# Layer pair 1 in seven products on pairs of token blocks, weight sums kept in DRAM

## The chip, the cores and the metric

One core of a Trainium2 chip runs the whole program. The metric is device time in microseconds (us) of that core; lower is better. The kernel before takes 1819.49 us, the median of three runs (1819.48 to 1819.55).

## The reference

Attention over pooled keys, then two gated layer pairs on its output, all in float32:

```
k_p, v_p = mean over 8 neighbouring positions of k, v   # 576 -> 72 keys
attn = softmax(q @ k_p^T / 8) @ v_p                     # batch 8, heads 8, head size 64
x = attn as 4608 tokens x 512
y = ((x @ w_a) * (x @ w_b)) @ w_out                     # 512 -> 1536 -> 512  (layer pair 1)
h = y @ w_in                                            # 512 -> 2048         (layer pair 2)
out = (h * clip(h + 3, 0, 6) / 6) @ w_out2              # 2048 -> 512
```

q, k and v come as float32, the weights as float64; the kernel decodes each weight from its two 32-bit halves.

## The kernel before

4608 tokens are 9 blocks of 512. Layer pair 1 is one loop over blocks j and over f, the 12 tiles of 128 columns of `w_a` and `w_b` (`step`, L670). x lies transposed: 4 chunks of 128 features on the partitions, 512 tokens in the free dimension, as a high part `xh` (float32r) and a low part `xl`; every weight tile is split in the same way. A product of two split numbers is three matmuls (`mm3`, L510): high x high, low x high, high x low. So a step is 4 chunks x 3 matmuls for `pa`, the same for `pb`, and 4 x 3 for y of the step before (`y_part`): 36 matmuls of 128x128 on 512 columns. y stays in four PSUM banks over the 12 f of a block and leaves them once (`y_store`). ScalarE copies `pa` and `pb` to SBUF (L695, L708), GpSimd multiplies them (L713), ScalarE rounds the product to its high part and GpSimd subtracts (L73, L74). Block 0 works in plain float32, four-pass matmuls; in it the weights are decoded. In block 1 they are split and stored to DRAM (`w1dram`), and from block 2 on loaded again at every step, `AHEAD = 3` steps ahead (L507).

Attention runs between the steps. A block has 4 or 5 chunks of up to 128 query rows; each has its transposes, scores, softmax, a second transpose and, for a piece of one or two chunks, the product with v (`pv`, L345), which writes `xh` and `xl`. Every one of these calls stands in a slot; there are 3 slots a step, 36 a block (`plan`, `at`, `place`), and `base` gives the slot at which a chunk begins: the chunks of block j run during block j - 1. From block 3 on the weights of layer pair 2 are staged too, an item per two steps (`w2_stage`, `w2_decode`, `w2_end`).

The order is the one in which the program is written (`manual_schedule`); every engine works through its own instructions in that order. All DMAs are issued by SP's queue (SyncE), in that order too: one that waits for its data, or for its slot in a pool, holds the ones behind it. A pool tag has a fixed number of slots; `wpool` has 28 of 4 KB per partition and serves weights, raw q and k and, in layer pair 2, nearly everything.

Layer pair 2 already works in seven products on two blocks at once: h and f are split in halves, `in_prod` computes the products 1, 2, 6, 5, 7, 3, 4 in three PSUM banks (Z, W, X), with sums of weights from DRAM (`wsd`) and sums of y made in the last pair of the superblock before (`s_make`), and `out_chunk` adds the output in SBUF (L865) after every pair of f tiles.

Of the kernel before, what the change touches and what calls it, by code (L numbers as in the profile page):

```python
# [25 lines left out]
def pooled_attention_then_two_moe_kernel(  # L26
# [34 lines left out]
    xpool = ctx.enter_context(tc.tile_pool(name="xpool", bufs=2))  # L61
    gpool = ctx.enter_context(tc.tile_pool(name="gpool", bufs=2))
    spool = ctx.enter_context(tc.tile_pool(name="spool", bufs=2))
# [6 lines left out]
    ydram = [dpool.tile([P, NCC, TB], F32, name=f"ydram{j}") for j in range(NB)]  # L70

# [34 lines left out]
    def x_tiles(j):  # L106
        if j not in xh_t:
            xh_t[j] = xpool.tile([P, NCC, TB], F32R if j else F32, tag="xh", name=f"xh{j}")
            xl_t[j] = xpool.tile([P, NCC, TB], F32R, tag="xl", name=f"xl{j}") if j else None
        return xh_t[j], xl_t[j]  # L110

    def load_tile(b, shape, name):


        if b == 0 or b >= 3:
            return wpool.tile(shape, F32, tag="w", name=name)
        return ld.tile(shape, F32, tag="ld", name=name)
# [8 lines left out]
    kpool, vpool = {}, {}  # L126

# [217 lines left out]
    def pv(pi, g):  # L345
# [11 lines left out]
        xh, xl = (x[:, 2 * g : 2 * g + 2, r : r + N] if x is not None else x for x in x_tiles(j))  # L357
# [24 lines left out]
    SLOTS = 3 * NF1  # L382
    plan = {}
# [4 lines left out]
    base = []  # L388
    for j in range(NB):
        n = len(block_chunks[j])  # L390
        for i, c in enumerate(block_chunks[j]):
            if j == 0:
                base.append(None)
            elif j == 1:
                base.append(4 * i + 6)
            else:
                base.append(SLOTS * (j - 1) - 8 + i * SLOTS // n)
    att_used = {}

# [10 lines left out]
    for c, (b, t0, n) in enumerate(chunks):  # L410
        pi, off = chunk_piece[c]
        s0 = base[c]
        near = b < 3
        if c in block_chunks[0]:
            continue
        if t0 == 0:
# [7 lines left out]
            for g in range(2):  # L424
                at(dma_at[1][g], v_dma, b, g)
                at(v_at[g], v_prep, b, g)
                at(v_at[g] + 1, v_write, b, g)
# [7 lines left out]
        if b == 0:  # L435
            place(s0, (q_tr, c))
        else:
            at(s0, q_tr, c)
        x = place(max(s0, done) + 1, (scores, c, 0), (scores, c, 1))
        at(x + 1, expo, c)  # L440
        at(x + 2, sums, c)
        at(x + 3, normal, c)
        x = place(x + 5, (at_main, c), (at_left, c))
        if off + n == pieces[pi][2]:
            for g in range(2):
                x = place(max(x + 1, s0 + 10 + g), (pv, pi, g))

    def run_slot(s):
        for fn, args in plan.pop(s, ()):
# [66 lines left out]
    def layer_in(o, w, xh, xl):  # L516
        for c in range(NCC):
            s = slice(c * P, (c + 1) * P)
            if xl is None:
                nc.tensor.matmul(o, w[:, s], xh[:, c], start=c == 0, stop=c == NCC - 1)  # L520
                continue
            mm3(o, w[:, 0, s], w[:, 1, s], xh[:, c], xl[:, c], c == 0, c == NCC - 1)


    yacc, later = {}, []
# [14 lines left out]
    def y_store(j, half):  # L540


        if j == NB - 1:
            t = wpool.tile([P, 2, TB], F32, tag="w", name="yl")
            nc.scalar.copy(t[:, 0], yacc[j][2 * half])
            nc.vector.tensor_copy(t[:, 1], yacc[j][2 * half + 1])
            nc.sync.dma_start(ydram[j][:, 2 * half : 2 * half + 2], t)
            return
        for c in (2 * half, 2 * half + 1):
            yo = spool.tile([P, TB], F32, tag="io", name="yo", bufs=2)  # L550
# [22 lines left out]
    def w2_decode(i):  # L573
        w2st[i] = w2st[i], spool.tile([P, 512], F32, tag="wst", name="w2f")
        decode_begin(w2st[i][1], w2st[i][0])
        decode(w2st[i][1], w2st[i][0])
# [93 lines left out]
    def step(j, f):  # L670
# [5 lines left out]
        i = NF1 * (j - 3) + f  # L676
        staged = i // 2 - 1 if 2 < i < 4 * NF2 + 2 and i % 2 else None
        stores, later[:] = list(later), []
        if j == 0:
            if f + 3 < NF1:  # L680
                w1_dma(f + 3)
        nj, nf = divmod(NF1 * j + f + 1, NF1)
# [4 lines left out]
        if 2 <= lj < NB:  # L687
            w1_load((lj, lf), lf, 0)
            w1_load((lj, lf), lf, 1)
        if 0 <= i < 4 * NF2 and i % 2 == 0:  # L690
            w2_stage(i // 2)
# [319 lines left out]
```

## Time and profile before

| | |
|---|---|
| median of the runs | 1819.49 us |
| the profiled execution: span | 1818.9 us |
| TensorE / VectorE / ScalarE / GpSimd busy | 1781.3 / 956.1 / 726.9 / 750.9 us |
| DMA | 328.71 MB, 181 GB/s over the span |

Busy times are those of one profiled execution. A matmul's record reaches past the start of the next one, so the time that a matmul costs is read from the distance of starts. "Idle before" is the time that an engine stood still just before an instruction, and the name behind it is what ended that. PEclk is the granted clock of TensorE as a share of 2.4 GHz.

### The profile page before, as it was taken

What the parts mean: (1) busy time and instruction counts of PE and PEld (TensorE: products, weight loads), DVE (VectorE), ACT (ScalarE), POOL (GpSimd) and SP (SyncE); (2) the same over time, 40 slices, a digit from 0 to 9 for tenths busy, and PEclk for the clock granted to TensorE, in tenths of its full rate; (3) what the DMA queues carried; (4) which work ended last, traced back from release to release, by engine and by line L of the source; (5) the groups of instructions that cost most, each with busy time, mean ns of one, the idle gap of its engine ahead of it and who ended that gap; (6) DMA issues with size and microseconds to landing.
All of it is one profiled execution on the core that took longest, in us unless ns stands there. A gap on an engine that the chain in (4) does not pass through costs nothing.

```text
span 1818.9 us, 23423 instructions
## 1 busy us (share of the span) xinstructions
PE 1781.3 (98%) x8148; PEld 1435.3 (79%) x8148; DVE 956.1 (53%) x1617; ACT 726.9 (40%) x1389; POOL 750.9 (41%) x653
## 2 busy tenths in 40 slices
PE   5999999999999999999999999999999999999998
PEld 4444788888888888888888878888888888888897
DVE  6787644323455345454332366685447445644645
ACT  4454443323333334333333355445325433433443
POOL 4545554333444444444343357464225223422322
PEclk8999999999999999999999999999999999999999
DMA  9652356635646548565545467556446543644483
GB/s 248 183 167 53 123 171 212 209 109 157 238 150 201 199 153 262 169 202 188 196 157 203 165 232 268 197 181 219 138 139 205 173 149 124 212 152 153 148 294 127
DMA packets 196260, 328.71 MB, mean 181 GB/s; under 512 B 86320, under 2 KB 107824, under 8 KB 196144
## 3 DMA queue, kind: packets, MB, share of 16 engines
q1 hardware_dynamic: 196144, 327.22, 55.2%
q8 instruction: 65, 1.06, 0.2%
q14 instruction: 51, 0.42, 0.1%
HBM read 264.24 MB, written 62.91 MB: 180 GB/s over the span
## 4 chain that ended last, share of the span: by engine, by line
PE 90%; DVE 5%; ACT 1%; issue 1%; SPq 0%; DMA 0%; POOL 0%; DVEq 0%; ACTq 0%
PE o L512 7%; PE o L513 7%; PE o L514 7%; PE pa L512 5%; PE pb L512 5%; PE pa L514 5%; PE pa L513 5%; PE y L512 5%; PE pb L513 5%; PE pb L514 5%; PE y L514 5%; PE y L513 5%; PE phZ L512 3%; PE phZ L513 3%; PE phZ L514 3%; PE sc L258 2%
## 5 line engine op out<-in xcount | busy, mean ns | idle before, releaser
L74 POOL TENSOR_TENSOR g<-r,g 128x512 fp32r<-128x512 f32 (+1 forms) x160 | 197.8, 1246 | 425.5 <-ACT g L73 255.9
L865 DVE TENSOR_TENSOR oacc<-o,oacc 128x512 f32<-128x512 f32 x252 | 172.3, 688 | 135.2 <-PE o L514 135.0
L713 POOL TENSOR_TENSOR asb<-asb,bsb 128x512 f32<-128x512 f32 x96 | 126.1, 1314 | 250.8 <-ACT bsb L708 217.7
L513 PE MATMUL o<-wo,g 128*128 128x512 f32 x576 | 224.4, 390 | 0.0
L514 PE MATMUL o<-wo,g 128*128 128x512 f32 x576 | 224.2, 389 | 0.0
L512 PE MATMUL o<-wo,g 128*128 128x512 f32 x576 | 211.6, 390 | 1.4 <-ACT g L73 1.2
L695 ACT COPY asb<-pa 128x512 f32<-128x512 f32 x108 | 63.3, 586 | 275.2 <-PE pa L514 231.0
L74 POOL TENSOR_TENSOR gl<-asb,gh 128x512 fp32r<-128x512 f32 x96 | 128.6, 1340 | 107.0 <-ACT gh L73 105.4
L512 PE MATMUL pa<-xh,wa 128*128 128x512 f32 x384 | 152.8, 398 | 0.0
L514 PE MATMUL pa<-xl,wa 128*128 128x512 f32 x384 | 149.8, 390 | 0.0
L513 PE MATMUL pa<-xh,wa 128*128 128x512 f32 x384 | 149.6, 390 | 0.0
L846 ACT ACTIVATE r<-hs 128x512 f32<-128x512 f32 (+1 forms) x120 | 69.0, 590 | 165.3 <-DVE hs L896 163.0
L708 ACT COPY bsb<-pb 128x512 f32<-128x512 f32 x108 | 63.3, 586 | 176.7 <-PE pb L514 149.3
L512 PEld LDWEIGHTS o<-wo,g 128*128 128x128 f32 x576 | 107.5, 188 | 23.9 <-ACT g L73 2.4
L514 PEld LDWEIGHTS o<-wo,g 128*128 128x128 f32 x576 | 108.2, 188 | 22.1
L513 PEld LDWEIGHTS o<-wo,g 128*128 128x128 f32 x576 | 108.2, 188 | 22.1
L512 PE MATMUL phZ<-Sh,wi 128*128 128x512 f32 (+1 forms) x320 | 117.5, 368 | 1.2 <-DVE hs L896 1.2
L513 PE MATMUL phZ<-Sh,wi 128*128 128x512 f32 (+1 forms) x320 | 117.7, 368 | 0.0
L73 ACT CAST g<-r 128x512 fp32r<-128x512 f32 (+1 forms) x160 | 91.9, 579 | 62.7 <-DVE r L847 62.6
L514 PE MATMUL phZ<-Sl,wi 128*128 128x512 f32 (+1 forms) x320 | 114.6, 368 | 0.0
L847 DVE SCALAR_TENSOR_TENSOR r<-r,hs 128x512 f32<-128x512 f32 (+1 forms) x120 | 92.5, 788 | 27.0 <-ACT r L846 26.7
L87 POOL TENSOR_TENSOR w2f<-w2f,w2st 128x512 int32<-128x512 int32 x32 | 42.5, 1328 | 135.7 <-DVE w2f L86 93.9
(1361 smaller groups left out, 4170.7 us busy)
## 6 DMA issues: line engine op xcount, KB each, us to landing
wi<-wsd SPq DMA_DIRECT2D x96, 512.0 KB
wo<-wod SPq DMA_DIRECT2D x64, 512.0 KB
wsd<-wi SPq DMA_DIRECT2D x24, 512.0 KB
kraw<-in_k_dram SPq DMA_DIRECT2D x32, 288.0 KB
out_dram<-oacc SPq DMA_DIRECT2D x36, 256.0 KB
vraw<-in_v_dram SPq DMA_DIRECT2D x32, 256.0 KB
ydram<-yo SPq DMA_DIRECT2D x32, 256.0 KB
w2st<-in_moe_w_in_dram SPq DMA_DIRECT2D x16, 512.0 KB
```

Source lines behind the costliest of these rows:

```text
L73: (hi_eng or nc.scalar.copy)(hi, src)
L74: (lo_eng or nc.gpsimd).tensor_tensor(lo, src, hi.bitcast(F32), ALU.subtract)
L87: nc.gpsimd.tensor_tensor(di, di, lo.bitcast(I32), ALU.add)
L512: nc.tensor.matmul(o, wh, xh, start=first, stop=False, skip_group_check=more)
L513: nc.tensor.matmul(o, wl, xh, start=False, stop=False, skip_group_check=more)
L514: nc.tensor.matmul(o, wh, xl, start=False, stop=last, skip_group_check=more)
L695: nc.scalar.copy(asb, pa)
L708: nc.scalar.copy(bsb, pb)
L713: nc.gpsimd.tensor_tensor(asb, asb, bsb, ALU.mult)
L846: nc.scalar.activation(r[:, :n], src, AF.Relu, bias=3.0)
L847: nc.vector.scalar_tensor_tensor(r[:, :n], r[:, :n], 6.0, src, ALU.min, ALU.mult)
L865: nc.vector.tensor_tensor(acc, o, acc, ALU.add)
```

## The change

Blocks 0, 1 and 2 (`PLAIN = 3`) stay as they are. Blocks 3 to 8 become three superblocks of two blocks (1024 tokens), and their gates are computed as in layer pair 2. The two halves of a superblock are its blocks; the 512 features are split in halves, and the 12 f tiles are taken in six pairs (p, p + 6). For each of the seven products `x_prod` runs twice, for `w_a` and for `w_b`, 6 matmuls each. The Z banks use the PSUM tag that `pa` and `pb` had, W, X and the y chunks share the four banks that y had.

- The sums of weights are made once by `t_make` in slots 48 to 114 (blocks 1 and 2 and the first steps of superblock 0): per pair seven casts on ScalarE, four sums on VectorE and seven subtractions, a third of them on GpSimd; 42 tiles of 0.5 MB go to DRAM (`tdram`). The decoded weights take a turn through DRAM for it (`abdram`).
- A tile of sums is loaded for every product, `LEAD = 3` products ahead (`ab_load`); `w_out` once per pair.
- x of blocks 3 to 8 goes to DRAM as attention makes it (`x_store`), without the subtraction for the low part, and comes back as four half tiles (`x_load`), from which `x_make` makes the seven sums with their low parts: for superblock 0 in slots 99 to 110, for the others during the last pair of the superblock before.
- y is no longer summed over f in PSUM: after each pair, eight chunks of 6 matmuls are evicted and added in SBUF by VectorE (`y_chunk`), spread over the next pair's products by `YWORK`.
- The slots of a pair are 12, one or two behind each half product (`hook`). Attention of blocks 3 and 4 now begins in slots 45 to 79, of 5 and 6 in 97 to 148, of 7 and 8 in 154 to 218, with one slot more between its parts. Staging of an item of layer pair 2 takes 6 slots.
- The first operands of layer pair 2 are made in the last pair of superblock 2 (`y_load` and two sums 16 slots before its end), in place of the last six steps of block 8.
- `xpool`, `gpool` and `spool` have one tag each, with 8, 7 and 4 slots.

The core of the diff:

```diff
+    SPAN2 = (26, 41)
+    SPANS = ((45, 79), (97, 148), (154, 218))
+    T_AT = [*range(48, 57), 72, *range(75, 82), *range(83, 90), *range(91, 98), *range(99, 106), *range(107, 115)]
...
+            for n, i in enumerate((1, 2, 4, 6, 5, 3, 7)):
+                if held:
+                    low()
+                t = wpool.tile([P, 2, 2, 256], F32R, tag="w", name=f"tt{p}_{i}")
+                nc.scalar.copy(t[:, 0], src[i])
+                if i in sums:
+                    nc.vector.tensor_tensor(*sums[i])
+                held = t, src[i], i
...
+    def x_evict(s, p, i):
+        za, zb_ = xb["Za"], xb["Zb"]
+        if i in (1, 6, 5):
+            for m in "ab":
+                xk[i, m] = tmp(F32, f"k{i}{m}")
+                nc.scalar.copy(xk[i, m], xb[("X" if i == 5 else "Z") + m])
+        due = split_due.pop() if split_due else None
+        if i in (2, 7, 3):
+            k, bank, key = {2: (1, "W", (0, 0)), 7: (5, "Z", (1, 1)), 3: (6, "X", (0, 1))}[i]
+            ta, tb = xk.pop((k, "a")), xk.pop((k, "b"))
+            nc.vector.tensor_tensor(ta, xb[bank + "a"], ta, ALU.add)
+            nc.vector.tensor_tensor(tb, xb[bank + "b"], tb, ALU.add)
+            nc.gpsimd.tensor_tensor(ta, ta, tb, ALU.mult)
+            split_due.append(((s, p) + key, ta))
+        elif i == 4:
+            ta = tmp(F32, "k4")
+            nc.scalar.copy(ta, za)
+            nc.vector.tensor_tensor(ta, zb_, ta, ALU.mult)
+            split_due.append(((s, p, 1, 0), ta))
+        if due:
+            key, t = due
+            g = wpool.tile([P, 2, TB], F32R, tag="w", name="g1")
+            split(g[:, 0], g[:, 1], t)
+            g1_t[key] = g
+
+    def y_chunk(s, p, h, c):
+        o = ps_acc.tile([P, TB], F32, tag="acc", name="y1")
+        cs = slice(c * P, (c + 1) * P)
+        for fi in range(2):
+            g, w = g1_t[s, p, fi, h], wo1_t[s, p][fi]
+            mm3(o, w[:, 0, cs], w[:, 1, cs], g[:, 0], g[:, 1], fi == 0, fi == 1)
...
+            (nc.scalar.copy if c % 2 else nc.vector.tensor_copy)(acc, o)
+        else:
+            nc.vector.tensor_tensor(acc, o, acc, ALU.add)
...
+    YWORK = (1, 1, 2, 1, 1, 1, 1)
...
+        for q, i in enumerate(ORDER):
+            n = 7 * (NP1 * s + p) + q
+            ab_load(n + LEAD)
+            if q == 0:
+                wo1_load(s, p)
+            if p == NP1 - 2 and q == 6 and not last:
+                x_load(s + 1)
+            x_prod(s, p, i, 0)
+            hook()
+            x_prod(s, p, i, 1)
+            x_evict(s, p, i)
...
+            for _ in range(YWORK[q] if work else 0):
+                y_chunk(*work.pop(0))
+            hook()
```

## Rows read from the trace of the kernel before

**Rows 1.** The page: span, and busy us (share) x instructions of each engine.
```profile
span 1818.9 us, 23423 instructions
PE 1781.3 (98%) x8148; PEld 1435.3 (79%) x8148; DVE 956.1 (53%) x1617; ACT 726.9 (40%) x1389; POOL 750.9 (41%) x653
```

**Rows 2.** The page: the chain that ended last, shares by engine.
```profile
PE 90%; DVE 5%; ACT 1%; issue 1%; SPq 0%; DMA 0%; POOL 0%; DVEq 0%; ACTq 0%
```

**Rows 3.** Busy us by stretch: PE, PEld, DVE, ACT, POOL; clock, DMA share, GB/s.
```profile
424.00:531.00 107.00, 105.92 (x505) 87.96 (x504) 47.25 (x95) 38.23 (x78) 43.10 (x40) 1.00 0.64 198
534.00:967.00 433.00, 431.78 (x2092) 359.49 (x2092) 193.43 (x390) 156.20 (x316) 187.26 (x167) 1.00 0.59 193
```

**Rows 4.** Timeline of TensorE: start us, us, then the matmul; three gate matmuls.
```profile
753.84 0.47 PE L512 MATMUL pb<-xh,sp(6, 0)_0_6628 128*128 128x512 f32 x1
...
966.96 0.39 PE L512 MATMUL pb<-xh,sp(7, 11)_0_8608 128*128 128x512 f32 x1
...
975.12 0.39 PE L512 MATMUL pb<-xh,sp(8, 0)_0_8674 128*128 128x512 f32 x1
```

**Rows 5.** VectorE by line and form: busy us, mean ns | idle before, its releaser.
```profile
L865 DVE TENSOR_TENSOR oacc<-o,oacc 128x512 f32<-128x512 f32 x252 | 172.3, 688 | 135.2 <-PE o L514 135.0
...
L91 DVE SCALAR_TENSOR_TENSOR w2f<-w2st,w2f 128x512 uint32<-128x512 uint32 x32 | 42.6, 1330 | 13.0 <-POOL w2f L87 12.9
...
L74 DVE TENSOR_TENSOR Sl<-yb,Sh 128x1024 fp32r<-128x1024 f32 x17 | 26.6, 1567 | 4.3 <-ACT Sh L73 4.0
...
L331 DVE TENSOR_TENSOR atl<-atm,ath 128x512 fp32r<-128x512 f32 x32 | 22.1, 692 | 103.5 <-ACT ath L330 103.3
...
L896 DVE TENSOR_TENSOR hs<-phW,kgl 128x512 f32<-128x512 f32 x32 | 22.0, 688 | 27.0 <-ACT kgl L891 13.1 <-ACT r L846 7.2 <-PE phW L514 6.7
...
L86 DVE TENSOR_SCALAR w2f<-w2f 128x512 uint32<-128x512 uint32 x32 | 13.7, 428 | 1.1
...
L85 DVE TENSOR_SCALAR w2f<-w2f 128x512 f32<-128x512 f32 x32 | 13.5, 422 | 106.2 <-ACT w2f L79 106.0
...
L74 DVE TENSOR_TENSOR wi<-sums,wi 128x512 fp32r<-128x512 f32 x9 | 9.2, 1034 | 0.5 <-ACT wi L73 0.5
...
L824 DVE TENSOR_TENSOR yT<-yb,yT 128x1024 f32<-128x1024 f32 x1 | 1.4, 1421 | 0.8 <-DMA yb<-ydram 0.8
...
L74 DVE TENSOR_TENSOR sp(1, 5)_1_2066<-raw,sp(1, 5)_1_2066 128x512 fp32r<-128x512 f32 x1 | 1.4, 1371 | 1.5 <-ACT sp(1, 5)_1_2066 L73 1.5
...
L74 DVE TENSOR_TENSOR sp(1, 6)_1_2142<-raw,sp(1, 6)_1_2142 128x512 fp32r<-128x512 f32 x1 | 0.7, 691 | 0.0
```

**Rows 6.** Busy times by 50 us: block 0, and the start of layer pair 2.
```profile
100.00:150.00 50.00, 47.59 (x159) 24.78 (x158) 40.88 (x82) 23.97 (x48) 26.69 (x25) 1.00 0.54 155
...
1050.00:1100.00 50.00, 48.77 (x216) 40.06 (x215) 32.23 (x37) 28.60 (x52) 31.33 (x27) 1.00 0.72 267
...
1200.00:1250.00 50.00, 49.85 (x220) 40.95 (x219) 36.87 (x43) 26.93 (x41) 26.77 (x15) 1.00 0.62 205
```

**Rows 7.** Busy times by 10 us, for the DMA's share and rate (the last two numbers).
```profile
590.00:600.00 10.00, 10.00 (x51) 8.07 (x50) 7.15 (x17) 5.02 (x12) 2.96 (x3) 1.00 0.48 100
600.00:610.00 10.00, 10.00 (x46) 8.29 (x45) 1.68 (x4) 2.97 (x5) 5.98 (x7) 1.00 0.98 361
```

**Rows 8.** GpSimd and ScalarE by line and form.
```profile
L74 POOL TENSOR_TENSOR gl<-asb,gh 128x512 fp32r<-128x512 f32 x96 | 128.6, 1340 | 107.0 <-ACT gh L73 105.4 <-DVE vraw L132 1.6
L713 POOL TENSOR_TENSOR asb<-asb,bsb 128x512 f32<-128x512 f32 x96 | 126.1, 1314 | 250.8 <-ACT bsb L708 217.7 <-PE y L514 21.0 <-PE sc L258 11.8
...
L891 ACT COPY kgl<-phX 128x512 f32<-128x512 f32 x32 | 18.7, 583 | 14.9 <-PE phX L514 14.7
```

**Rows 9.** Timeline of SP's queue: start us, us that the issues took, xcount.
```profile
539.92 7.73 SPq L223 DMA_DIRECT2D qraw<-in_q_dram  x16
...
689.42 7.39 SPq L182 DMA_DIRECT2D vlraw<-in_v_dram  x6
...
699.07 13.18 SPq L223 DMA_DIRECT2D qraw<-in_q_dram  x16
```

More of the change, by code (lines that the diff above doesn't have):

```diff
@@ L126, in pooled_attention_then_two_moe_kernel, with flush, x_store @@
     kpool, vpool = {}, {}
+    x_done, xo_due, xo_t, later = {}, [], {}, []
+    def flush():
+        for dst, src in later:
+            nc.sync.dma_start(dst, src)
+        later.clear()
+    def x_store():
+        if xo_due:
+            nc.sync.dma_start(*xo_due.pop(0))
     def sum8(dst, t, eng=None):
@@ L386, in at, with spread @@
         plan.setdefault(slot, []).append((fn, args))
[L388 to L397, printed above, removed]
+    def spread(cs, first, last):
+        n = len(cs)
+        return [first + i * (last - first) // max(1, n - 1) for i in range(n)]
+    base = [None] * len(block_chunks[0])
+    base += [4 * i + 6 for i in range(len(block_chunks[1]))]
+    base += spread(block_chunks[2], *SPAN2)
+    for s in range(NSUP):
+        base += spread(block_chunks[PLAIN + 2 * s] + block_chunks[PLAIN + 2 * s + 1], *SPANS[s])
     att_used = {}
+    WIDE = block_chunks[PLAIN][0]
     def place(slot, *calls):
@@ L540, in y_store @@
     def y_store(j, half):
[L543 to L548, printed above, removed]
         for c in (2 * half, 2 * half + 1):
-            yo = spool.tile([P, TB], F32, tag="io", name="yo", bufs=2)
+            yo = spool.tile([P, TB], F32, tag="io", name="yo")
             if c % 2 == 0:
@@ new lines, in pooled_attention_then_two_moe_kernel, with x_load, x_make, piece @@
+    xr, sx = {}, {}
+    def x_load(s):
+        while xo_due:
+            x_store()
+        for h in range(2):
+            assert x_done[PLAIN + 2 * s + h] == 2 * TB
+        for k, h in ((0, 0), (0, 1), (1, 1), (1, 0)):
+            t = wpool.tile([P, 2, TB], F32, tag="w", name=f"xr{s}_{k}{h}")
+            nc.sync.dma_start(t, xdram[PLAIN + 2 * s + h][:, 2 * k : 2 * k + 2])
+            xr[s, k, h] = t
+    def x_make(s):
+        v00, v01, v11, v10 = (xr.pop((s, k, h)) for k, h in ((0, 0), (0, 1), (1, 1), (1, 0)))
+        due = []
+        def piece(i, src, lo_eng):
+            h = wpool.tile([P, 2, TB], F32R, tag="w", name=f"xSh{s}_{i}")
+            lo = wpool.tile([P, 2, TB], F32R, tag="w", name=f"xSl{s}_{i}")
+            nc.scalar.copy(h, src)
+            sx[s, i] = (h, lo)
+            due.append((lo, src, h, lo_eng))
+        def low():
+            lo, src, h, eng = due.pop()
+            eng.tensor_tensor(lo, src, h.bitcast(F32), ALU.subtract)
+        t2 = wpool.tile([P, 2, TB], F32, tag="w", name=f"xT{s}")
+        piece(1, v00, nc.vector)
+        eng = nc.gpsimd if s else nc.vector
+        eng.tensor_tensor(t2, v11, v01, ALU.subtract)
+        yield
+        low()
+        nc.vector.tensor_tensor(v00, v01, v00, ALU.subtract)
+        eng.tensor_tensor(v01, v11, v00, ALU.subtract)
+        piece(2, v10, nc.vector)
+        yield
+        low()
+        piece(6, v01, nc.vector)
+        eng.tensor_tensor(v10, v10, v01, ALU.subtract)
+        yield
+        low()
+        piece(5, v00, nc.gpsimd)
+        yield
+        low()
+        piece(7, t2, nc.vector)
+        yield
+        low()
+        piece(3, v11, nc.vector)
+        yield
+        low()
+        piece(4, v10, nc.gpsimd)
+        yield
+        low()
@@ new lines, in x_prod @@
+    def x_prod(s, p, i, m):
+        bank = ("Z" if i in (1, 6, 7, 4) else "W" if i == 2 else "X") + "ab"[m]
+        first = i in (1, 2, 5)
+        if first:
+            if bank[0] == "Z":
+                xb[bank] = ps.tile([P, TB], F32, tag="ab", name="p" + bank)
+            else:
+                xb[bank] = ps_acc.tile([P, TB], F32, tag="acc", name="p" + bank)
+        o, w = xb[bank], ab_t[s, p, ORDER_OF[i]]
+        sh, sl = sx[s, i]
+        for c in range(2):
+            cs = slice(c * P, (c + 1) * P)
+            mm3(o, w[:, 0, m, cs], w[:, 1, m, cs], sh[:, c], sl[:, c], first and c == 0, c == 1, not first)
@@ L917, in p2_begin @@
+    P2_AT = (NP1 - 2, 6)
     def p2_begin():
```

257 lines of the change are left out of this document (197 added, 60 removed).

## The prediction

> **What bounds the kernel now.** I read the busy table first: TensorE works 98% of the span, no other engine more than 53% [rows 1]. The chain that ended last is TensorE for 90%, spread over the matmul lines [rows 2]. Then the stretches: from 534 to 967 us, the middle of layer pair 1, TensorE is busy 431.78 of 433 us at granted clock 1.00 (the 2.4 GHz level) [rows 3]. Time here falls only if matmuls fall away or are slowed less, and no other engine has to be made faster. A matmul on 512 columns costs what lies between starts, not its "busy" 390 ns: from the first gate matmul of step (7, 11) at 966.96 to that of (8, 0) at 975.12 there are 36 matmuls, no attention between them, so 8.16 / 36 = 0.2267 us [rows 4]. From (6, 0) at 753.84 to (8, 0) are two blocks, 221.28 us, 110.6 each [rows 4]; 12 x 8.16 = 97.9 are steps, 12.7 are attention, and at 40 chunks in 9 blocks that is 2.9 us a chunk.
>
> **What it removes.** Two blocks by two f tiles now cost 4 steps x 36 = 144 matmuls. The new pair needs 7 products x 2 matrices x 6 = 84 for the gates and still 8 x 6 = 48 for y: 132. Three superblocks x six pairs x 12 = 216 matmuls, x 0.2267 = 49.0 us off the path. y must now leave PSUM after every pair, and the products must be evicted and added: that, the sums of weights and of x, and their DMA are the price.
>
> **VectorE in the superblocks.** Per pair: six adds of a PSUM bank (2, 7 and 3, both matrices) at 0.688, as L896, one product for 4 at the same price, eight adds of y at 0.688, as L865 [rows 5]: 15 x 0.688 = 10.3 us, six pairs 62. An item of w2 staging costs 0.42 + 0.43 + 1.33 = 2.18 [rows 5], 12 in 72 units. An attention chunk: VectorE has 193.4 us in 534:967 [rows 3]; less 24 items x 2.18 = 52 and some 5 of y copies, 136 for 17.4 chunks, 7.9; the subtraction of x (the same form as L331, 0.69 [rows 5], twice per piece) goes for blocks 3 to 8, so 7.3. The slot lists put eleven chunks into superblock 0 (97 to 148 by 6.4, then every 8), five into superblock 1, none into 2. Superblock 0 then holds 80 + 62 + 26, 9 of the last weight sums and 9.5 for the next x pieces (five subtractions at 1.567 and one more of that size [rows 5]), together 186 us of VectorE; TensorE needs 6 x 132 x 0.2267 = 179.6 + 11 x 2.9 = 211. That is 88%. Superblock 1: 133 of 194, 69%. Superblock 2: some 100 of 180.
> What does 88% cost? No stretch of before has it with VectorE in the eviction path. The nearest from below: 1050:1100 and 1200:1250, where layer pair 2 runs this same form of seven products, with VectorE at 64% and 74%, and TensorE loses 1.23 and 0.15 of 50 us [rows 6]. From above: 100:150 in block 0, VectorE 82%, TensorE loses 2.41 of 50, 5% [rows 6]. Over 211 us that bounds it by 1 and 10.5; I take 8, nearer to the 82% row because 88% is beyond it.
>
> **Blocks 1 and 2.** Block 1 takes nine chunks instead of four (66 us), its old splits (12 x about 2.1 = 25) and the sums of pair 0: seven subtractions, a third of them on GpSimd, and four sums of 128x512, about 8.7 x 1.03 = 9 us [rows 5]; 101 of 97.9 + 26 = 124 us, 81%. Block 2: five chunks (37), four pairs of sums (36), x pieces (five at 1.567, four sums of at least 1.4: 14), 88 of 112 us, 79%. Here the gates are evicted by ScalarE and multiplied by GpSimd; VectorE delays only attention's own matmuls, which the slot lists leave a slot or two more. From 0 (hidden as in 534:967) to the 5% of block 0, 6 us; I take 2.
> In block 2 the DMA is dense: 28 stores of weight sums of 0.524 MB (14.7), five pairs of raw tiles (5.2), nine steps of layer loads at 1.05 (9.4), x (2.1), three sum tiles (1.6), attention loads and x stores (4.9), y (1.0): 39 MB in 112 us, 348 GB/s, where the best 10 us give 361 [rows 7]. What is late first are the stores, which hold slots of the 28 work tiles, so that ScalarE's casts of the next sum wait, and behind them the evictions of pa and pb in its queue. Bounds: 0, since layer loads run three steps (27 us) ahead, and 11, if each of two or three q loads takes the rate down to the 100 GB/s of 590:600 [rows 7] for 10 us; I take 2.
>
> **Last pairs.** In the last pair of superblocks 0 and 1 the x pieces come, in that of 2 seven subtractions for layer pair 2 (1.567 each) and the first weight sums (ten instructions near 1.03, and y's last sum) beside 10.3: 32 of 30 us there. That work had six steps before. Between 0 (as in superblock 1, where the same pair has VectorE at 69%) and 5 (the 2 over, and the in-order wait of one large subtraction, 3.2 [rows 5]); I take 2.
> **What I cost at nothing.** Per pair GpSimd has three products and four subtractions, 3 x 1.314 + 4 x 1.340 = 9.3 us of 30, ScalarE seven bank copies at 0.583 and four casts, some 6.6 [rows 8]; TensorE hides both. The tightest gate is that of product 3: its adds follow the end of 3b, the cast stands behind the copy of 4a, which waits no longer than for 4b, 4.1 us later (y chunk 1.36, product 4 2.72); copy 0.58, cast 0.6 and subtraction 1.34 end it at 6.6, and the first y that reads it comes after another chunk and the next product 1, at 8.2. That leaves 1.5 us; where GpSimd or ScalarE is later than that, TensorE waits for the rest. Bank Z is free after the last product in the same way: 2.7 us for a copy and a product, 1.3.
>
> **Sum.** 8 + 2 + 2 + 2 = 14. The execution has a span of 1818.9, 0.6 below the median of 1819.5: 1818.9 - 49.0 + 14 + 0.6 = 1784.5.
>
> **A rule against it.** The split of weight part 1, two SBUF inputs on VectorE, takes 0.691 us or 1.371 [rows 5], while adds with a PSUM input stay at 0.688. The Trainium skill (SBUF — State Buffer, "Who interferes with whom") states that a VectorE instruction with two SBUF inputs contends with a GpSimd one that reads SBUF, and that the loser blocks; the trace agrees in both halves. By it the new evictions keep their price and the weight sums pay the dear price whenever GpSimd runs: 52 instructions at 1.371 make 71 us instead of 54.
>
> **Rivals.** *VectorE becomes the bound from block 1 to superblock 0.* It serves its queue in order; before, it idled 103.3 us before the 32 large subtractions of L331, waiting for ScalarE [rows 5], 3.2 each. If these waits stay under load, superblock 0 needs 186 + 11 x 3.2 = 221 of 211, block 1 101 + 29 = 130 of 124; with the 52 instructions of the sums at 1.371 instead of 1.03 (18) and the terms that are left (4), 10 + 6 + 18 + 4 = 38 are lost: 1808.5. For it: the loads above. Against: under load ScalarE is ahead and such waits shrink.
> *All of it arrives.* Layer pair 2 loses almost nothing with the same form [rows 6]. Then 1818.9 - 49.0 + 0.6 = 1770.5, and 2.3 less if the small losses of 424:531 and 534:967 [rows 3] go too.
> *Slower: the loads of weight sums come late.* Place: superblocks 0 and 1, one SP queue. Each product needs 0.5 MB that is issued three products ahead, 3 x 18.9 x 0.2267 = 12.8 us, 17 if SP has run one ahead; before it was three steps, 27 us. A q load holds the queue for 7.73 to 13.18 us, one of v's remainder 7.39, and once both stood within 23 us [rows 9]. With landing of 1.5 us (0.524 MB at 361 GB/s), three such neighbours cost 23 + 1.5 - 17 = 7.5 each and eight single q loads 13.2 + 1.5 - 12.8 = 1.9: 38. With the 14 above and 11 more when the stores of block 2 are late, 63 are lost against 49: 1833. It decides from 3.2 us a load on (35 over eleven). Against: the eleven are spread over some 400 us, and a late load is followed by early ones. The x pieces go out and back by the same queue (12 x 1.05 MB, each store two slots behind ScalarE's copy); a store that waits there holds the sum tiles behind it, within the same 3.2 us.
> The q loads have packets of 128 bytes. The Trainium skill (DMA: Bandwidth & Descriptors, "Why small descriptors are slow (HBM only)") charges about 3 cycles a packet beside one per 32 bytes; by that a piece of 0.5 MB would take 7/4 of 1.45, an estimate of 2.5 us, and this rival would vanish. The rows with 7.73 to 13.18 differ from it, so I keep the rival.
>
> **How the numbers follow.** The forecast 0.50; with losses between 5 and 28 us, inside its bounds (1 to 32.5), it reaches from 1775.5 to 1798.5. All of it 0.20, VectorE as the bound 0.20, the slow loads 0.07, a cancelling mixture within 0.2% 0.03; 0.2% is about what a measurement can tell. So faster 0.90, same 0.03, slower 0.07. The range 1770 to 1809 leaves out a twentieth at the low end, the dearer half of the VectorE case and the slow loads: 2 in 10.
>
> **What would show it.** TensorE's count falls by 216 less the records missing. In the changed trace, superblock 0 at 219 us, superblock 1 near 196, superblock 2 near 182. TensorE's waits in superblock 0 should name VectorE (bank adds, y adds), at 8 us together; if they name the DMA of the sum tiles, the third rival is right; if VectorE is over 95% busy there, the first. The prediction is wrong if layer pair 2 or block 0 change by more than 2 us, or if the superblocks run above 0.2267 us a matmul with no wait shown.

## The result, and the profile after

The changed kernel takes 1842.54 us, the median of four runs (1839.58 to 1850.19), against 1819.52 before in the same comparison: ratio 1.0131, 95% interval 1.0109 to 1.0153. It is slower; the forecast was 1784.5. The profiled execution is the longest of the four (1850.19, span 1848.3). The stages below are read from it, so they explain some 7.6 us more than the median has.

The page of the changed kernel: busy time by engine; then the first and the granted-clock line of the 40 slices; then the chain that ended last.

```profile
PE 1759.7 (95%) x7932; PEld 1407.4 (76%) x7932; DVE 1167.5 (63%) x1903; ACT 752.4 (41%) x1434; POOL 801.6 (43%) x662
...
PE   5999999997798998999999999999999999999998
...
PEclk8999999999999999999999999999999999999999
...
PE 80%; DVE 9%; DMA 5%; issue 2%; SPq 1%; ACT 1%; POOL 1%; DVEq 0%; ACTq 0%; POOLq 0%
```

The 216 matmuls are gone, exactly: 8148 records became 7932 [rows 1]. Two things ate the 49.0 us they cost. Idle time of TensorE (span less busy) rose from 37.6 to 88.6, by 51.0; and its busy time fell by only 21.6, because 27.4 us went into matmuls that ran longer. Together 78.4, which is 1848.3 - (1818.9 - 49.0).

Where: stage by stage, beside what TensorE's own work costs there: 0.2267 us a matmul, and 2.9 a chunk of attention. A chunk's parts lie in different stages, so they are counted from the trace, each at its share of a chunk's TensorE time in blocks 3 to 8 before (scores 0.36, second transposes 0.22, products with v 0.42). The first stretch ends with the first gate matmul of block 1's second step, the others with that of the next stage; layer pair 2 is taken from its first matmul into bank Z (`phZ`, at 1088.64; before at 1072.13), ahead of which 12 others of its matmuls already ran (before 8). "Idle" is span less busy, beyond that of the same stretch before.

| stage | after | TensorE's work | lost | of it idle | forecast loss |
|---|---|---|---|---|---|
| block 0 and one step | to 204.58 | 199.9 as before + 1.1 chunks, 3.1 | 1.6 | 0.1 | 0 |
| the rest of blocks 1, 2 | 248.0 | 214.8 as before + 3.0 chunks, 8.7 | 24.5 | 15.1 | 4 |
| superblock 0 | 243.9 | 756 matmuls, 11.3 chunks: 204.1 | 39.8 | 26.3 | 8 |
| superblock 1 | 207.2 | 792 matmuls, 5.9 chunks: 196.7 | 10.5 | 6.1 | 0 |
| superblock 2 | 184.9 | 792 matmuls and 12 of layer pair 2: 182.3 | 2.7 | 2.3 | } 2 |
| layer pair 2 | 759.7 | 746.8 as before + 32 matmuls, 7.3 | 5.6 | 3.6 | } |

The sum is 84.7. Blocks 3 to 8 of the kernel before had lost 6.3 in the same way (657.4 us for 2600 matmuls and 21.3 chunks, 2.3 of it idle), which the forecast carried along; that leaves the 78.4. The first row shows that blocks 0 to 2 did not quite stay as they were: the slots of block 2's attention moved too (`SPAN2`), so that 24 matmuls of attention more lie in the first stretch (597 records instead of 573).

Stretches of the changed kernel, as in [rows 3]: blocks 1 and 2 together; the worst step of block 1; the change to superblock 0; then pairs 0, 2 and 3 of superblock 0; a pair of superblock 2; and five us before and after 578.69.

```profile
204.58:452.61 248.03, 232.95 (x1126) 191.76 (x1125) 162.70 (x293) 111.28 (x228) 122.08 (x106) 0.97 0.76 250
265.00:285.76 20.76, 14.06 (x62) 10.80 (x59) 18.09 (x31) 7.22 (x16) 10.78 (x11) 0.84 0.54 160
423.13:452.61 29.48, 21.46 (x88) 15.88 (x87) 23.52 (x30) 13.67 (x22) 14.93 (x10) 0.94 0.73 253
452.61:498.79 46.18, 34.73 (x154) 26.84 (x152) 33.94 (x60) 19.12 (x39) 25.67 (x20) 0.89 0.89 294
538.69:579.25 40.56, 35.44 (x174) 29.27 (x173) 26.69 (x53) 12.29 (x24) 16.60 (x16) 0.96 0.67 207
579.25:622.14 42.89, 40.26 (x194) 33.76 (x195) 29.50 (x59) 15.45 (x36) 14.21 (x14) 0.94 0.81 237
...
996.02:1025.94 29.92, 29.92 (x133) 24.77 (x132) 13.05 (x21) 8.55 (x15) 12.09 (x10) 1.00 0.57 211
573.69:578.69 5.00, 0.35 (x1) 0.18 (x1) 4.86 (x8) 0.62 (x1) 4.94 (x5) 0.74 0.57 178
578.69:583.69 5.00, 4.56 (x13) 3.69 (x14) 2.83 (x6) 2.06 (x6) 0.37 (x1) 0.58 0.98 326
```

A pair without attention takes 29.92 us, 132 x 0.2267, with nothing lost: the seven-product form itself does what was forecast. VectorE's share over pair 2 is only 66% (26.69 of 40.56), yet in the five us before 578.69 VectorE and GpSimd are busy throughout (4.86 and 4.94) and TensorE is busy for 0.35. Much of the loss lies in such bursts. VectorE's queue at that place (start, duration, line, operation):

```profile
572.22 0.68 DVE L1142 TENSOR_TENSOR ya<-y,ya 128x512 f32<-128x512 f32 x1
572.82 1.40 DVE L151 TENSOR_TENSOR kraw<-kraw 72x512 f32<-72x512 f32 x1
574.25 1.37 DVE L152 TENSOR_TENSOR kraw<-kraw 72x256 f32<-72x256 f32 x1
575.65 1.01 DVE L153 TENSOR_TENSOR kp<-kraw 72x128 f32<-72x128 f32 x1
576.59 0.68 DVE L100 SCALAR_TENSOR_TENSOR w2f<-w2st,w2f 128x512 uint32<-128x512 uint32 x1
577.20 0.44 DVE L282 TENSOR_REDUCE mx<-sc 128x4 f32<-128x288 f32 x1
577.67 0.46 DVE L283 TENSOR_TENSOR sm<-sc,mx 128x288 f32<-128x288 f32 x1
...
578.90 0.71 DVE L151 TENSOR_TENSOR kraw<-kraw 72x512 f32<-72x512 f32 x1
579.64 0.42 DVE L152 TENSOR_TENSOR kraw<-kraw 72x256 f32<-72x256 f32 x1
```

And TensorE's queue at the same place; the bracket is the idle time before a matmul and what ended it.

```profile
578.27 0.35 PE L169 MATMUL ktp<-ident,kp 72*128 72x72 f32 x1 [4.62 <-DVE sm L283]
...
580.67 0.63 PE L555 MATMUL pZa<-xSh,ab 128*128 128x512 f32 x1
581.10 0.63 PE L556 MATMUL pZa<-xSh,ab 128*128 128x512 f32 x1
...
583.07 0.39 PE L555 MATMUL pZb<-xSh,ab 128*128 128x512 f32 x1
583.30 0.39 PE L556 MATMUL pZb<-xSh,ab 128*128 128x512 f32 x1
```

To be read here: a batch of attention begins, and its k sums stand in consecutive slots between evictions. One k sum takes 1.40 + 1.37 + 1.01 us while GpSimd has work, and 0.71 + 0.42 in the first two parts of the next, while GpSimd has almost none (0.37 of 5 us). TensorE has a tiny transpose (`ktp`) in its queue that needs a PSUM slot; the slot comes free with the softmax's subtraction (`sm`), which stands behind those sums in VectorE's queue. So TensorE stands 4.62 us before `ktp`, with product matmuls behind it. Then the product matmuls start 0.43 us apart, the 1.2 GHz level, until about 583, where they return to 0.23; the granted clock of the stretch is 0.58. So this stall is paid twice. The contention is the rule of the Trainium skill that the prediction weighed (SBUF — State Buffer, "Who interferes with whom"); these rows agree with it: 1.37 us beside a busy GpSimd, 0.42 beside an idle one.

TensorE's waits from 452 to 700 us (what waited, for whom, us in total, times, longest):

```profile
PE ktp L169 <- DVE sm L283: 5.1, 2, 4.6
PE atm L347 <- DVE sm L283: 3.5, 1, 3.5
PE ktp L169 <- DVE atl L350: 2.9, 1, 2.9
PE sc L277 <- DVE atl L350: 2.8, 2, 2.7
...
PE pWa L555 <- DMA ab<-tdram: 2.2, 1, 2.2
```

Of the 26 us, 16.2 end with VectorE, 6.2 with ScalarE or GpSimd, 3.7 with a load. The long ones are attention's own matmuls; the bank adds and y adds that the forecast watched hardly appear.

### The profile page after: what moved, and what is told of

The parts are those of the page before. It is cut to its first block, busy times and chain, and to the rows that moved or that the text cites. A ratio compares the mean times of both kernels' runs of the same rounds, so it can differ in the third digit from the quotient of the medians.

```text
span 1848.3 us, 23716 instructions
## 1 busy us (share of the span) xinstructions
PE 1759.7 (95%) x7932; PEld 1407.4 (76%) x7932; DVE 1167.5 (63%) x1903; ACT 752.4 (41%) x1434; POOL 801.6 (43%) x662
## 2 busy tenths in 40 slices
DMA packets 220808, 385.36 MB, mean 208 GB/s; under 512 B 90128, under 2 KB 118288, under 8 KB 220688
## 4 chain that ended last, share of the span: by engine, by line
PE 80%; DVE 9%; DMA 5%; issue 2%; SPq 1%; ACT 1%; POOL 1%; DVEq 0%; ACTq 0%; POOLq 0%
PE o L555 7%; PE o L556 7%; PE o L557 7%; PE y L557 4%; PE y L555 4%; PE y L556 4%; PE phZ L555 4%; PE phZ L557 3%; PE phZ L556 3%; DMA ab<-tdram 2%; PE sc L277 2%; PE pa L564 2%; PE phX L557 2%; PE phX L555 2%; PE phX L556 2%
## 5 line engine op out<-in xcount | busy, mean ns | idle before, releaser
L83 POOL TENSOR_TENSOR g<-r,g 128x512 fp32r<-128x512 f32 (+1 forms) x160 | 205.4, 1294 | 421.3 <-ACT g L82 373.7
L1142 DVE TENSOR_TENSOR ya<-y,ya 128x512 f32<-128x512 f32 x120 | 82.1, 688 | 125.0 <-PE y L557 125.0
L887 ACT ACTIVATE r<-hs 128x512 f32<-128x512 f32 (+1 forms) x120 | 70.8, 590 | 201.0 <-DVE hs L937 199.9
L888 DVE SCALAR_TENSOR_TENSOR r<-r,hs 128x512 f32<-128x512 f32 (+1 forms) x120 | 98.6, 821 | 27.1 <-ACT r L887 27.1
L557 PE MATMUL y<-g,wo 128*128 128x512 f32 x288 | 112.2, 390 | 1.7 <-POOL g L83 1.7
L555 PE MATMUL y<-g,wo 128*128 128x512 f32 x288 | 112.2, 389 | 0.0
L556 PE MATMUL y<-g,wo 128*128 128x512 f32 x288 | 112.1, 389 | 0.0
L1117 POOL TENSOR_TENSOR k5a<-k5a,k5b 128x512 f32<-128x512 f32 x18 | 23.2, 1287 | 130.6 <-DVE k5b L1116 122.7
L555 PEld LDWEIGHTS phZ<-Sh,wi 128*128 128x128 f32 x320 | 60.1, 188 | 15.7 <-ACT kgl L932 2.5
L556 PEld LDWEIGHTS phZ<-Sh,wi 128*128 128x128 f32 x320 | 60.2, 188 | 10.7
L557 PEld LDWEIGHTS phZ<-Sl,wi 128*128 128x128 f32 x320 | 60.2, 188 | 10.2
```

Source lines behind the costliest of these rows:

```text
L83: (lo_eng or nc.gpsimd).tensor_tensor(lo, src, hi.bitcast(F32), ALU.subtract)
L555: nc.tensor.matmul(o, wh, xh, start=first, stop=False, skip_group_check=more)
L556: nc.tensor.matmul(o, wl, xh, start=False, stop=False, skip_group_check=more)
L557: nc.tensor.matmul(o, wh, xl, start=False, stop=last, skip_group_check=more)
L887: nc.scalar.activation(r[:, :n], src, AF.Relu, bias=3.0)
L888: nc.vector.scalar_tensor_tensor(r[:, :n], r[:, :n], 6.0, src, ALU.min, ALU.mult)
```

## Experiments

All were timed against the kernel before on the same chip; its medians there were 1819.5 to 1820.4, so that differences between two experiments are good to about 1 us at best. "Pairs" are lengths in us of the six pairs of superblock 0; in the changed kernel 46.2, 39.9, 40.6, 42.9, 35.3, 39.1. Theory V: VectorE is late. Theory L: the loads of sum tiles are late. Theory S: making and storing the sums costs.

**Without the sums.**

```diff
-            later.append((abdram[f][:, 0], rawa_t[f][:, f % 2]))
-            later.append((abdram[f][:, 1], raw_t[f][:, 0]))
-            nc.sync.dma_start(m, tdram[p][q])
+            nc.sync.dma_start(m.rearrange(...), w1dram[(7 * p + q) % NF1][0])
-    for x in T_AT:
-        at(x, next, maker_t, None)
```

> Left out: the sums of weights are not made (no casts, sums, subtractions, stores to tdram, no round trip of the decoded weights); each product loads a tile of the same size that is there anyway. All else as in the changed kernel (1842.5 us; profiled span 1848.3). Theory V (TensorE waits in order for VectorE, whose queue is too full from block 1 to the start of superblock 1): 54 to 71 us of VectorE go, nearly all in blocks 1 and 2; the step at 265 us that takes 20.8 and those of 17.2 and 12.3 before superblock 0 fall to 9 to 11, and the first pair of superblock 0 from 46 to below 40; pairs 1 to 4 of superblock 0 stay at 37 to 43. Total 1815 to 1825. Theory L (loads and stores late in SP's queue and DMA): the 22 MB of stores go, so the steps before superblock 0 fall too, but the step of 20.8 in block 1 stays (few stores there), and pairs 1 to 4 fall by 2 to 3 each, since they start with no backlog. Total 1820 to 1830. If the sums cost little, total above 1835.

1813.36 us (ratio 0.9966, 0.9953 to 0.9979): the sums cost 29 us. Superblock 0 begins at 433.78 instead of 452.61; pairs 34.5, 35.2, 40.6, 42.8, 36.2, 38.7. The first two are shorter by 16.4 together, the others little changed, so most of superblock 0's loss is not the sums'.

**Without attention's computing in blocks 3 to 8**, all loads and x stores kept (its chunks' calls return at once; ScalarE stores a constant tile).

> Left out: the computing of attention for the tokens of blocks 3 to 8 (and of k and v from batch 3 on); every load of q, k and v and every store of x stays, ScalarE stores a constant tile as x. TensorE loses some 25 chunks x 2.9 = 73 us of matmuls, so the total says little; the pairs do. Theory V: superblock 0 and 1 have pairs of 29.9 to 31, except the first (the sums' last pair) and the last. Theory L: the q loads still hold the queue 8 to 13 us each, so pairs of superblock 0 stay at 33 or more, with waits of TensorE for ab tiles above 10 us in all.

1779.98 (0.9783). Pairs 46.3, 38.4, 29.9, 43.9, 30.0, 29.9: most pairs come to 29.92, and the five long ones among the eighteen wait for loads. TensorE's waits from 300 to 1000 us:

```profile
PE pZa L562 <- DMA ab<-tdram: 15.9, 7, 5.4
PE pWa L562 <- DMA ab<-tdram: 13.0, 2, 7.8
PE y L562 <- ACT yo L597: 10.3, 1, 10.3
...
PE pXa L562 <- DMA ab<-tdram: 6.0, 1, 6.0
```

34.9 us of late loads, where the changed kernel shows 6.5 and most of its idle time in superblock 0 ends with VectorE. Theory L looks like a second limit right behind the first; the runs with spread sums below bear it out.

**Loads five products ahead** (`LEAD = 3` to 5) **and k and v sums of batches 3 to 7 on GpSimd** (`sum8(kp, t, nc.gpsimd if b > 2 else nc.vector)`, v likewise).

> Sum tiles are loaded five products ahead instead of three; nothing else. Theory V: within 4 us of the changed kernel (1842.5), either side. Theory L: 8 to 15 us faster, 1828 to 1834, and no wait of TensorE for ab tiles (5.0 + 1.5 us before).

> The pooling sums of k and v of batches 3 to 7 go to GpSimd, which has them of batch 0 already: some 70 us leave VectorE, some 85 come to GpSimd. Theory V: 8 to 20 us faster (1822 to 1834), the pairs of superblock 0 at 34 to 38. Theory L: within 3 us. If GpSimd's queue is the tight one instead (the gate's product and low part wait there), slower by 5 or more, with TensorE waiting for g1 tiles.

The earlier loads gave 1846.97 (1.0146): no gain, as theory V says. GpSimd gave 1836.78 (1.0084), with pairs 47.0, 37.6, 40.5, 43.1, 36.8, 37.7: the 6 us come before superblock 0 (it begins at 439.06), which itself takes 242.7 instead of 243.9. Inside it the waits change their names: 7.3 us end with VectorE, 6.9 with a load, 6.1 with ScalarE and 4.3 with GpSimd.

**Less load, or the same load spread.** The first run takes some 4 us of VectorE a pair out of superblock 0 (149.5 us busy there instead of 173.6); the second moves the batch sums apart and leaves every instruction (batch 5's raw k tiles take slots of the pool `ld` instead of `wpool`); the third does both.

```diff
-                i, ph = divmod(24 * 3 * s + 4 * 3 * p + u, 6)
+                i, ph = divmod(24 * 3 * s + 4 * 3 * p + u - W2_FROM, 4)
...
+    W2_FROM = 66
...
+            if b == 5:
+                k_at, v_at = [74, 82, 90, 98], [s0 - 3, s0, s0 + 3]
+            elif b > 5:
+                k_at, v_at = [s0 - 24 + 5 * i for i in range(NP)], [s0 - 3, s0 + 1, s0 + 5]
```

> The decoding of the second layer pair's weights (5 VectorE operations a stage, some 3.3 us of VectorE in each pair of superblock 0) begins at slot 66 of the superblocks instead of slot 0, at every 4th slot instead of every 6th; all else is as in the changed kernel. So superblock 0 loses about 3.3 us of VectorE work in each pair, and the k and v sums at the batch changes stand as closely as before. Theory A (the total of VectorE in a pair is the bound): pairs 1 to 5 of superblock 0 (39.9, 40.6, 42.9, 35.3, 39.1 us) each lose about 3 us, superblock 1 gives 3 back: 1829 us. Theory B (the bursts at the batch changes hold TensorE, whatever the total): a shorter backlog only where a burst comes, 2 us in each of pairs 1 to 3, nothing elsewhere: 1836 us. Theory L (loads of the sum tiles): no change by VectorE, but less DMA in superblock 0 (0.2 MB less a stage): 1838 us.

> The k sums of batches 5 to 7 stand 5 slots apart (those of batch 5 in the free slots 74, 82, 90, 98 before superblock 0) instead of in 4 slots in a row, and their v sums 3 to 4 slots apart instead of 1; the work is the same. Theory B (bursts): the waits of ktp, sc and pv for VectorE at the batch changes go, pairs 1 to 4 of superblock 0 come to 33 to 36 us, the first two of superblock 1 to 34: 20 to 25 us less, 1820 us. Theory A (total of VectorE in the pair): only the k sums of batch 5 (8 to 10 us of VectorE moved ahead of superblock 0, into block 2, which then pays for them): 1838 to 1843 us.

> The weights' decoding late (from slot 66) and the spread k and v sums of batches 5 to 7 together. Theory B: little beyond the spread sums alone, 1817 us. Theory A: as with the late decoding alone, 1828 us. Where both hold, total and bursts, the two gains add: 1806 to 1810 us, with pairs 1 to 4 of superblock 0 at 31 to 33 us.

Late decoding: 1844.23 (1.0134), no gain; superblock 0 is 12.9 us shorter in its profile (231.0) and the later superblocks give 9.0 of it back. Spread sums: 1828.21 (1.0047), 14.3 us less with VectorE just as busy (1168.1 us, 1167.5 in the changed kernel); pairs 46.0, 35.2, 35.6, 38.4, 35.6, 39.1. Both: 1833.88 (1.0075). So it pays to move the bursts apart, as theory B said, though less than the 20 to 25 expected; theory A's gain (to 1829) did not come from the total alone, though the total has a part in superblock 0, which the late decoding did shorten. Pairs 1 to 3 of the kernel with spread sums:

```profile
496.75:531.92 35.17, 35.17 (x172) 28.58 (x172) 24.54 (x54) 15.46 (x34) 14.54 (x15) 1.00 0.84 258
531.92:567.48 35.56, 35.21 (x175) 29.28 (x174) 24.01 (x48) 12.98 (x27) 12.51 (x12) 1.00 0.71 215
567.48:605.86 38.38, 37.78 (x193) 31.38 (x192) 29.09 (x59) 14.57 (x30) 16.92 (x18) 1.00 0.79 252
```

TensorE is busy nearly throughout, at clock 1.00. Pair 0 stays long, and its waits are now for loads (TensorE's waits from 450 to 690 us):

```profile
PE pZa L559 <- DMA ab<-tdram: 5.7, 1, 5.7
PE pXa L559 <- DMA ab<-tdram: 3.4, 1, 3.4
PE sc L277 <- DVE atl L350: 3.3, 3, 2.8
```

**Eased further**: the sums of batches 3 and 4 and k of batch 5 on GpSimd, the transposes one or two slots later; with late decoding, and then without.

> Late decoding and spread sums as in the run before, and besides the sums of batches 3 and 4 (k and v) and k of batch 5 on GpSimd instead of VectorE, and the transposes of the k sums one or two slots later, so that TensorE comes to them when they are long done. If VectorE's load in blocks 1 and 2 is what makes these blocks late, superblock 0 begins some 10 us sooner than with both edits alone: 1798 us. If the stores and the GpSimd queue of the weight sums are, GpSimd now makes it worse there: 1815 us.

> The spread k and v sums of batches 5 to 7, the sums of batches 3 and 4 and k of batch 5 on GpSimd, the transposes of the k sums later; the decoding of the second layer pair's weights where it was. With the decoding late as well this took 1821.5, and between the two kernels with spread sums alone the late decoding cost 5.7 (1833.9 against 1828.2): 1816 us if the three edits add, 1822 if the decoding's lateness cost nothing here.

1821.53 (1.0007) and 1820.20 (1.0004, 0.9994 to 1.0013): the same as the kernel before, within the interval. The second is called the eased kernel from here; spread sums and easing together take back 22 us. The late decoding makes no difference here that the runs can tell, where it cost 5.7 above.

**Sums computed but not stored** (the `later.append` of `tdram` left out, other tiles loaded).

> The changed kernel with the weight sums computed as in it (their loads, copies, sums and low parts), but not stored: 42 stores of 0.5 MB are left out, and the superblocks load other weights of the same size that an earlier stage stored, so that the output is not the reference's. The kernel with neither sums nor stores took 1813.4 us, the changed kernel 1842.5. If the computing (some 40 us of VectorE in blocks 1 and 2, the GpSimd queue) is what costs these 29 us: 1838 us, superblock 0 still beginning at 448 to 452 us. If the stores and their DMA time are (0.76 of 16 engines busy in blocks 1 and 2, against 0.59 without): 1818 us, superblock 0 beginning at 436 us.

1825.99 (1.003): of the 29 us the stores are 16.5; the other 12.6 are the computing and the raw tiles' turn through DRAM (`abdram`), which this run keeps. Both theories were half right.

**Stores on ScalarE's queue** (from block 1 on `nc.scalar.dma_start` in `flush` and in `step`): on the changed kernel, on the eased one, and there with loads five ahead.

> The changed kernel with only the same stores on ScalarE's queue from block 1 on; nothing else differs. If the order of the one queue costs what the stores cost (16.5 us): 1828 us. If the bytes do, or VectorE's bursts hide it: 1842 us. If ScalarE is held by the stores' waits: 1850 us.

> As the run before, and the stores that are put off until their data should be ready (the sum tiles, the split weights, the decoded weights, the last y) issued on ScalarE's queue instead of SP's, from block 1 on; the same bytes. If the order of the one queue is what makes the stores dear (loads wait behind stores that wait for VectorE): superblock 0 begins 8 us sooner and its first pair loses its wait for ab: 1804 us. If the bytes are: no change, 1816. If ScalarE is held by stores that wait for VectorE or GpSimd: evictions come late, 1825 or more.

> As the eased kernel with stores on ScalarE's queue, and the sum tiles loaded 5 products ahead instead of 3. Where the loads now come in time, no change (within 2 us); where the first pair of superblock 0 still waits for them, 5 us less.

1854.91 (1.0191), 1834.68 (1.0089) and 1843.36 (1.0132): 12.4 and 14.5 us worse with the stores parted off, and worse still with earlier loads. ScalarE's waits from 395 to 505 us in the first of them:

```profile
ACT ath L349 <- DMA qraw<-in_q_dram: 14.0, 1, 14.0
ACT bsb L744 <- DMA xr<-xdram: 7.6, 1, 7.6
ACT xSh L1033 <- DVE xr L1048: 7.5, 1, 7.5
```

ScalarE's copies of attention and of gate banks now wait at transfers, which they did not in the changed kernel, where `ath` waited for TensorE (6.2 in the same place) and no `bsb` for a DMA. From 467.42 three stores of sums take 10.18 us on ScalarE's queue, and the copy behind them is `ath` at 477.64: a store at the head of an engine's queue holds that engine. Some 5 us of the loss arise only in layer pair 2 (764.8 us instead of 759.7). In the changed kernel the same waits stand on SP's queue, from 200 to 460 us:

```profile
SPq L740 <- DVE tt L993: 14.0, 8, 4.3
...
SPq L242 <- DMA tdram<-tt: 7.9, 7, 2.1
```

The Trainium skill (DMA: Bandwidth & Descriptors, "Issuing engines are not separate DMA queues") says that a second issuing engine saves only issue time, since the same 16 DMA engines do the work. The result agrees: nothing was saved, and ScalarE paid.

**Fewer sums to compute.** 18 of the 42 tiles hold a plain quarter of w_a and w_b, whose split block 1 makes anyway; they are stored from there instead of being split anew. In the first run from block 1's tiles, in the second with loads five ahead, in the third from the tiles in use in block 2, in the fourth with batch 2's sums on GpSimd and loads four ahead as well. The sums that are left got new slots in all four (`T_AT`, 28 instead of 46).

```diff
+    def quarters(f, m, w):
+        for i, c in ((1, 0), (2, 256)) if f < NP1 else ((4, 256),):
+            dst = tdram[f % NP1][ORDER_OF[i]].rearrange("p (a b) f -> p a b f", b=2)[:, :, m]
+            later.append((dst, w.bitcast(F32)[:, :, c : c + 256]))
...
-            for n, i in enumerate((1, 2, 4, 6, 5, 3, 7)):
+            for n, i in enumerate((5, 6, 7, 3)):
```

> Spread k and v sums, those of batches 3 to 5 on GpSimd and their transposes later, with the decoding of the second layer pair's weights where it was; and of the 42 tiles of weight sums the 18 that hold a plain quarter (a11, a12, a22) are stored out of the split weights that block 1 makes anyway, instead of being copied and split anew: 18 ScalarE copies and 18 low parts of 128x1024 less in blocks 1 and 2, the same bytes stored, but 9.4 MB of them in block 1 instead of block 2. If computing the sums is what makes block 2 late: superblock 0 begins at 430 to 435 us (442.6 with late decoding and no such sharing), 1805 us. If the stores are: 440 us and 1818 us, block 1 now losing what block 2 gains.

> As the run before, with the sum tiles loaded 5 products ahead instead of 3. In the changed kernel this gained nothing (1847.0), since VectorE was late first. If, with VectorE's bursts eased, the loads of sum tiles are the next thing late (the wait of pZa for ab of 5.9 to 6.9 us in pair 0 of superblock 0): 6 to 10 us less than with 3, 1797 us. If the queue of the loads waits for free buffers (the slots of the weight pool) and not for its turn: no gain or a loss, as before.

> The eased kernel (1820.2) with the 18 plain quarters of the sum tiles stored out of the split weights, as in the run with sharing (1824.4), but from the tiles in use in block 2 instead of those being made in block 1. VectorE loses 18 low parts of 128x1024, ScalarE 18 copies, the bytes stay, and the stores lie where they lay in the changed kernel. If the place of the stores was what spoiled the sharing: block 1 as in the eased kernel, superblock 0 beginning at 432 to 436 us instead of 442.6: 1811 us. If DMA is the limit of block 2 whatever VectorE does: 442 and 1820.

> As the run before, batch 2's k and v sums on GpSimd too, and the sum tiles loaded 4 products ahead instead of 3. If the slow step of block 1 (at 262 us, TensorE waiting 4.7 us for q transposes behind those sums) and the two loads of pair 0 (4.7 and 4.4 us) are each independent of the rest: 10 us less than the run before, 1801 us. If GpSimd's sums slow VectorE's by as much as they spare it, and loads wait for buffers: no gain, 1811.

1824.38, 1824.60, 1825.42 and 1824.39, all 4.2 to 5.2 above the eased kernel: the gains expected did not come. VectorE has 10 us less (1140.4 against 1150.4), and superblock 0 begins later, at 456 to 459 instead of 442.6, while its pair 0 shrinks from 47.7 to 35 to 39: its second pair begins between 490.3 and 495.1 in all five. What holds block 2 there, by the chain, is transfers. In the third run:

```profile
400.00:450.00 50.00, 33.11 (x132) 26.26 (x133) 29.85 (x38) 15.76 (x28) 19.87 (x15) 0.79 0.91 313
```

```profile
399.52 6.55 DMA ra<-abdram
...
417.22 8.65 DMA tdram<-tt
...
426.25 7.22 DMA tdram<-tt
```

(The first fence is a stretch, the second the chain of waits: start, duration, piece.) The DMA engines are 0.91 busy at 313 GB/s, and the chain runs through loads of raw tiles and stores of sums. The quarters go out in 1 KB pieces, so that the kernel moves 228009 packets instead of 220808; whether this, the bytes alone or the new slots make the limit was not separated.

**Both causes away**: the eased kernel without the sums.

> The eased kernel (1820.2) with the weight sums, their stores and the round trip of the raw weights left out, as in the first experiment, and other weights of the same size loaded in their place, so that the output is not the reference's. If bursts and sums are independent, the 29.1 us of the sums come off: 1791 us, superblock 0 beginning near 428 us, its first pair at 33 us. If the easing already gave back part of what the sums cost (VectorE's load in blocks 1 and 2 is common to both): 1800 us. If loads from DRAM are a limit of their own, with waits for ab in several pairs as when attention's computing was left out: 1805 us.

1796.75 (0.9872, 0.9855 to 0.9888), between the first two expectations. The stretch of blocks 1 and 2 takes 226.6 us against TensorE's 223.5, with 1.2 idle; superblock 0 218.5, still 14.4 above its 204.1: 9.8 idle, 5.7 of it at loads, and the rest in matmuls that take longer than priced. The waits (TensorE, 429 to 690 us):

```profile
PE pXa L559 <- DMA ab<-w1dram: 4.4, 1, 4.4
PE sc L277 <- DVE atl L350: 3.3, 3, 2.7
PE pZa L559 <- DMA ab<-w1dram: 1.3, 1, 1.3
```

The four medians together: changed 1842.5, eased 1820.2, no sums 1813.4, both 1796.8. Easing is worth 22.3 with the sums and 16.6 without, the sums 29.1 and 23.4; 5.7 us belong to both; that this is where the sums' VectorE work lies beside the bursts is likely, but not shown. Of the 72 us between the forecast without any loss (1770.5) and the changed kernel, bursts and sums are 45.8; by its profile the last run still spends more than TensorE's own work in superblock 0 (14.4), layer pair 2 (5.4) and superblock 2 (4.3). No kernel that computes the reference came out ahead of the kernel before.

## Why the prediction was wrong, by its steps

- **What it removes**: right. 216 matmuls fewer, and 29.92 us for a pair without attention. The bookkeeping was off in one place: superblock 0 was given 6 x 132 matmuls, but its first pair has only the 12 of block 2's last step as y, and the last pair's 48 run in layer pair 2 (48 there instead of 12). That is no time, but it makes the test "layer pair 2 or block 0 change by more than 2 us" a wrong one: layer pair 2 changed by 12.9, 7.3 of it moved work, and the stretch of block 0 by 4.7, 3.1 of it moved attention.
- **VectorE in the superblocks**: the step that failed. Its work was as forecast: the durations of its instructions in superblock 0 add up to 186.0 us, forecast 186 (neighbours overlap, so that they cover 173.6, 85% of TensorE's 204.1). What failed is the price of that load: the loss was 39.8 and not 8. The step priced a mean share by stretches of other stages [rows 6], and its upper bound came from a row with 82%, less than the 88% that it had to bound. Here batch sums come in four consecutive slots, between transposes, softmax and evictions, and TensorE's queue holds small matmuls of attention that need their results. Moving those sums apart, without one instruction fewer, gave 14.3 us back, and the rest of the easing 8.0.
- **Blocks 1 and 2**: 24.5 instead of 4. Sums and their traffic are the larger cause here: without the sums the stretch is 16.2 us shorter (231.9), and eased as well it loses 3.1. The single prices were right or high: 27 low parts at 0.88 and 24 sums at 0.78 us are 42.5 us on VectorE, where 54 stood. The DMA was foreseen as dense and given 2 us, of bounds that went to 11; the stores cost 16.5 in the whole program.
- **The clock** was in no term. Of the 27.4 us by which matmuls ran longer, some 18 are large matmuls whose next one starts 0.38 us or more later, most at the 0.43 of the 1.2 GHz level (92 in the changed trace, 6 in the one before), and 5.4 are attention's own. They follow most of the long stalls, not all: after 2.22 us at 506.15 and 2.28 us at 907.49 the spacing stayed at 0.23.
- **Last pairs**: 2 forecast; superblock 2 and layer pair 2 lost 8.3. Superblock 1 lost 10.5, in its first five pairs; its last pair, with the x pieces for superblock 2, took 29.92, as forecast.
- **What was costed at nothing**: GpSimd's and ScalarE's gate chain was free, as said, in the pairs without attention; 29.92 shows it. In superblock 0 a wait of 2.6 us ends with ScalarE's `g`.
- **Rivals**: "VectorE becomes the bound" (1808.5) named the engine and the place but not the way; VectorE's waits before the large subtraction, priced at 35 us in superblock 0, were 6.3 there, and VectorE was never 95% busy over a stage. "Loads of weight sums come late" (1833) was nearest in time and wrong as the first cause: five products ahead gained nothing. It is the second limit, seen once VectorE is out of the way. In the changed kernel its waits are 6.5 us.

Still open: why the product and attention matmuls of superblock 0 take longer than priced even without sums and bursts, how much of superblock 0's loss is VectorE's total and how much its bursts, and why the runs of the changed kernel spread over 10.6 us where the kernel before spreads over 1.7.

## What to carry to other kernels

Where one in-order engine feeds small matmuls that stand in TensorE's queue among large ones, price the densest few slots and not the mean share: take the queue's backlog slot by slot and ask which of TensorE's instructions meets it. Where the rows show half-clock matmuls after a stall, add them to its price. And before one bound is lifted, ask which one lies just behind it: here the spread sums gave 14.3 us where 20 to 25 were expected, and the waits that came forward in pair 0 were 9.1 us of loads.

## What the runs showed of the hardware

- The same addition of two SBUF tiles of 72x256 took 0.42 us in all 16 cases with no GpSimd instruction beside it, and 1.15 to 2.50 us in 15 of the 16 with one; over all 32 the mean rose from 688 ns before to 931.
- After a stall of 4.62 us the product matmuls started 0.43 us apart for 3 us (579.82 to 582.80) before the spacing was 0.23 again.
- The stores' 22 MB of sums cost 16.5 us of a program whose DMA engines are 0.63 busy on average; in the stretch of blocks 1 and 2, where most of the sums are made, they are 0.76 busy.
